# Sixteen buffers for row numbers and twenty for y in a fused convolution and mixture-of-experts kernel

## The chip, the cores and the metric

The kernel runs on one core of a Trainium2 chip. The metric is the device time of one execution in microseconds (us), the median of several runs; lower is better. The engines are named as in the profile: PE is TensorE (matmuls; PEld its weight loads), DVE is VectorE, ACT is ScalarE, POOL is GpSimd, SP (SPq) is SyncE, which here only issues DMAs.

## The reference

For 8 sequences of 3584 tokens with 192 features, a causal convolution of 7 taps with weights of its own for every token and head is computed, and its result goes through a mixture of 8 experts of which every token uses one:

```python
w = softmax(weight_gen)                                   # over the 7 taps
attn = einsum('bshk,bskhg->bshg', w, windows_of_7(x))     # 8 heads of 24
logits = attn @ w_gate                                    # 28672 tokens, 8 experts
e = argmax(logits); g = softmax(logits)[e]
out[token] = g * (relu(attn[token] @ w1[e]) @ w2[e])      # 192 -> 1024 -> 192
```

## The kernel before

The tokens are cut into 16 stages of 14 x 128. For a stage, `conv` (lines 344 to 365) multiplies and adds the 7 taps on VectorE, in instructions over half or all of a stage's rows. `tops` and `halves` (367 to 386) split the result into two f16 parts, which stand in one of three tiles `rows`. `turn`, `products`, `route1`, `counts` and `route2` work out the expert of each token and its place in a scratch table in DRAM, `scr`, in which the rows of an expert stand together. `scatter` (455) is a GpSimd DMA that writes 128 rows to their places, 14 of them a stage. `table` (489) makes from the counts a list of blocks of 256 rows of one expert that are complete; the stages 1 to 14 have 7 blocks each, the last one the rest.

A block is loaded by `load` (551), all of it issued from SyncE's queue in this order: the expert's weights w1 into one of three tiles `wt` (lines 560, 561), the block's rows transposed into one of three tiles `xb` (564), and its row numbers and gates into `mt` (570). The second half of the weights, w2, is issued by `seconds` (581) a little later, when the block before no longer needs that place. `Block.first` (596) multiplies by w1 on TensorE in four steps of two 128-column parts and `hh` is relu of that, on ScalarE (609). `low` (612) makes `hl`, what `hh` lost by rounding: for the early stages on TensorE and ScalarE (616, 617), later on VectorE (619). `second` (624) multiplies `hh` and `hl` by w2. `out` (639) writes each half of the block, 128 rows, with its gate into a tile `y` on ScalarE (642), and a GpSimd DMA (643) scatters it to the rows of the output that `mt` names. So a buffer of `mt` is free again, and one of `y` too, when that scatter has read it.

The order of the work on VectorE, ScalarE, TensorE and SyncE is written out by two generators, `produce` (the stages) and `consume` (the blocks), which a loop at the end of the kernel draws from by estimated times. GpSimd executes what it issues in order as well, so an output scatter can stand behind a stage's row scatters and the small operations of lines 327 to 180. The convolution ends about 1010 us into the span and the routing of the last stage about 1065 us; from there on TensorE runs through the blocks that are left.

Of the kernel before, what the change touches and what calls it, by code (L numbers as in the profile page):

```python
# [9 lines left out]
I32 = mybir.dt.int32  # L10
# [5 lines left out]
P = 128  # L16
# [32 lines left out]
TW0, TWE, TWU = 18.0, 8.0, 1.0  # L49
BLK, NEG = 16.6, 0.21  # L50
LAG2, LAG0, LAGN, LAGL = 2, 4, 1, 4
HHB, HLB, YB = 6, 6, 12
AV = 4.0
NZ = [0] * 5 + [5] * 1 + [8] * 10
FINE = 8
# [24 lines left out]
def conv_moe_kernel(ctx: ExitStack, tc: tile.TileContext, x, wgen, wg_in, w1, w2, out):  # L80
# [19 lines left out]
    def raw(i):  # L100
        return getattr(i, "ins", i)
# [346 lines left out]
    def no_dep(i, *groups):  # L448
        for g in groups:
            tc.declare_no_dep(i, group=g, reason="rows are disjoint")  # L450
# [94 lines left out]
    def written(i, s):  # L545

        info = mybir.DependencyInfo(mybir.DependencyClass.Sync, mybir.DependencyReason.DATA)
        for k in scats[s] + (zeros if s == nchunk - 1 else []):
            tc.add_manual_dep(i, k.name, info, reason="rows of the stage")

    def load(s, tb, g, bs):
        nj = bs // P
        ffn = pools[0]
        with tc.issue_after(loaded[-1]) if loaded else ExitStack():
            rv = SP.value_load(tb[0:1, 0, g:g + 1], min_val=0, max_val=TRASH + 256 - bs)
            ev = SP.value_load(tb[0:1, 1, g:g + 1], min_val=0, max_val=E - 1)
        wt = wts[len(loaded2) % len(wts)]
        loaded2.append(None)
        seconds()
        SP.dma_start(out=wt[:, F:4 * F], in_=wsc[bass.ds(ev, 1), :, F:4 * F].rearrange("o p c -> p (o c)"))  # L560
        SP.dma_start(out=wt[0:64, 0:F], in_=wsc[bass.ds(ev, 1), 0:64, 0:F].rearrange("o p c -> p (o c)"))
        xb = ffn.tile([P, 3 * 512], F16, name="xb", bufs=3)
        xv = xb[:, 0:3 * bs].rearrange("p (a b) -> p a b", a=3)
        i = raw(SP.dma_start_transpose(out=xv, in_=scr[bass.ds(rv, bs), 0:384]))
        later = [f"scat{k}" for k in range(s + 1, nchunk)] + ([] if s == nchunk - 1 else ["zero"])
        no_dep(i, *later)
        written(i, s)
        tc.add_to_no_dep_group("loads", i)
        mt = ffn.tile([P, 4, 2], I32, name="mt", bufs=8)
        i = raw(SP.dma_start(out=mt[:, 0:nj, :], in_=scri[bass.ds(rv, bs), 192:194].rearrange("(j p) c -> p j c", p=P)))  # L570
        no_dep(i, *later)
        written(i, s)
        tc.add_to_no_dep_group("loads", i)
        loaded.append(i)
        halfway.append((wt, ev))
        return wt, xv, mt

    def seconds():
        while halfway:
            wt, ev = halfway.pop(0)  # L580
            SP.dma_start(out=wt[:, 4 * F:WW], in_=wsc[bass.ds(ev, 1), :, 4 * F:WW].rearrange("o p c -> p (o c)"))
# [213 lines left out]
    def consume():  # L795
# [8 lines left out]
        def ahead(n, k):  # L804
            while len(ready) < k and n + len(ready) < len(todo):
                s, i, b, bs = todo[n + len(ready)]
                if s not in avail or (ready and t < avail[s]):
                    break
                ready.append(load(s, seg_tabs[s][i], b, bs))
# [28 lines left out]
        def rest(i):  # L838
            if i < len(skip):
                loaded.clear()  # L840
                with tc.If(cnt > skip[i][2]):
                    for s, j, b, bs in skip[i:i + NSS]:
                        blk = Block(load(s, seg_tabs[s][j], b, bs), bs, (0,) * NF)
                        seconds()
                        for k in range(blk.steps):
                            step(blk, k)
                        blk.gates()
                        step()
                    rest(i + NSS)
# [51 lines left out]
```

## Time and profile before

| | |
|---|---|
| median of 3 runs | 1263.31 us (1262.53 to 1265.07) |
| the profiled execution | 1258.3 us |
| its span, first to last instruction | 1256.6 us |
| busy in the span: PE, DVE, ACT, POOL | 1131.6, 1062.3, 708.1, 793.4 us |
| mean granted TensorE clock | 0.964 |

The rows in the section further down come from that one execution; times in them count from the start of its span. A row of a timeline has the start, the duration, the engine, the line of the kernel, the operation, what it writes and reads, how many instructions the row merges, and in brackets the idle time of the engine before it and what ended it. A row of waits has the engine and the line that waited, what it waited for, the total in us, the times, and the longest.

### The profile page before, as it was taken

What the parts mean: (1) busy time and instruction counts of PE and PEld (TensorE: products, weight loads), DVE (VectorE), ACT (ScalarE), POOL (GpSimd) and SP (SyncE); (2) the same over time, 40 slices, a digit from 0 to 9 for tenths busy, and PEclk for the clock granted to TensorE, in tenths of its full rate; (3) what the DMA queues carried; (4) which work ended last, traced back from release to release, by engine and by line L of the source; (5) the groups of instructions that cost most, each with busy time, mean ns of one, the idle gap of its engine ahead of it and who ended that gap; (6) DMA issues with size and microseconds to landing.
All of it is one profiled execution on the core that took longest, in us unless ns stands there. A gap on an engine that the chain in (4) does not pass through costs nothing.

```text
span 1256.6 us, 31171 instructions
## 1 busy us (share of the span) xinstructions
PE 1131.6 (90%) x11784; PEld 1014.4 (81%) x11784; DVE 1062.3 (85%) x1421; ACT 708.1 (56%) x1299; POOL 793.4 (63%) x611
## 2 busy tenths in 40 slices
PE   1485588999999998799999999999999999999997
PEld 0143277898887897689999999999989899999996
DVE  8998999999999999889999999999999865333332
ACT  5878664868776775545555455555544354333332
POOL 3227534658889897888878686886858563521222
PEclk9886798999999999999999999999999999999999
DMA  9749697998969969899999999999997999999992
GB/s 324 213 161 296 218 304 180 269 244 272 282 184 268 261 204 266 248 273 290 309 273 306 267 278 289 284 287 257 290 246 223 277 251 274 302 287 254 255 247 69
DMA packets 211946, 323.03 MB, mean 257 GB/s; under 512 B 138894, under 2 KB 158463, under 8 KB 209744
## 3 DMA queue, kind: packets, MB, share of 16 engines
q1 hardware_dynamic: 190000, 276.01, 78.8%
q0 software_dynamic: 21792, 44.99, 12.3%
q8 instruction: 94, 1.54, 0.5%
q14 instruction: 60, 0.49, 0.2%
HBM read 237.87 MB, written 61.03 MB: 238 GB/s over the span
## 4 chain that ended last, share of the span: by engine, by line
DVE 47%; PE 29%; DMA 9%; issue 7%; SPq 3%; ACT 3%; POOL 2%; POOLq 0%; DVEq 0%; ACTq 0%
DVE tmp L358 14%; DVE acc L363 14%; PE po L635 13%; DVE hl L619 5%; PE p L602 3%; PE p L606 3%; PE p L603 3%; PE p L605 3%; PE p L604 3%; DMA out_dram<-y,mt 3%; DVE acc L358 3%; DVE rows L384 3%; DMA xb<-scr 2%; DMA scr<-rows,pos 1%; DMA wt<-wsc 1%
## 5 line engine op out<-in xcount | busy, mean ns | idle before, releaser
L643 POOL DMA_INDIRECT out_dram<-y,mt x230 | 351.0, 1526 | 275.4 <-ACT y L642 215.9
L609 ACT ACTIVATE hh<-p 128x512 f16<-128x512 f32 x460 | 275.3, 599 | 391.4 <-PE p L606 376.0
L456 POOL DMA_INDIRECT scr<-rows,pos x224 | 360.9, 1611 | 121.5 <-issue 61.2
L635 PE MATMUL po<-wt,hh 128*128 128x192 f16 x3680 | 366.8, 249 | 0.0
L619 DVE SCALAR_TENSOR_TENSOR hl<-p,hh 128x512 f16<-128x512 f32 x334 | 225.1, 680 | 148.7 <-ACT hh L609 148.4
L635 PEld LDWEIGHTS <-hh 128*128 128x128 f16 x3680 | 316.2, 99 | 3.7
L363 DVE TENSOR_TENSOR acc<-acc,tmp 128x1344 f32<-128x1344 f32 (+1 forms) x168 | 290.7, 1747 | 1.0
L358 DVE TENSOR_TENSOR tmp<-xin,wgt 128x1344 f32<-128x1344 f32 (+1 forms) x168 | 290.6, 1746 | 0.9
L602 PE MATMUL p<-xb,wt 128*128 128x256 f16 x920 | 251.9, 274 | 39.3 <-DMA xb<-scr 32.4
L606 PE MATMUL p<-xb,wt 128*128 128x256 f16 x920 | 252.2, 274 | 0.0
L605 PE MATMUL p<-xb,wt 128*128 128x256 f16 x920 | 252.2, 274 | 0.0
L603 PE MATMUL p<-xb,wt 128*128 128x256 f16 x920 | 252.0, 274 | 0.0
L604 PE MATMUL p<-xb,wt 128*128 128x256 f16 x920 | 252.0, 274 | 0.0
L635 PE MATMUL po<-wt,hl 128*128 128x192 f16 x1840 | 228.8, 247 | 0.0
L635 PEld LDWEIGHTS <-hl 128*128 128x128 f16 x1840 | 165.3, 98 | 7.9
L602 PEld LDWEIGHTS <-wt 128*128 128x128 f16 x920 | 90.3, 98 | 42.4 <-issue 24.2
L603 PEld LDWEIGHTS <-wt 128*128 128x128 f16 x920 | 90.2, 98 | 29.6 <-issue 14.6
L399 ACT ACTIVATE xt<-p 128x1024 f16<-128x1024 f16 x96 | 86.5, 925 | 37.7 <-PE p L398 37.7
L617 ACT ACTIVATE hl<-p 128x512 f16<-128x512 f32 x126 | 75.7, 601 | 53.9 <-PE p L616 53.8
L604 PEld LDWEIGHTS <-wt 128*128 128x128 f16 x920 | 90.4, 98 | 11.0
L606 PEld LDWEIGHTS <-wt 128*128 128x128 f16 x920 | 90.4, 98 | 11.0
L605 PEld LDWEIGHTS <-wt 128*128 128x128 f16 x920 | 90.4, 98 | 11.0
(123 smaller groups left out, 1056.4 us busy)
## 6 DMA issues: line engine op xcount, KB each, us to landing
wt<-wsc SPq DMA_DIRECT2D x115, 768.5 KB
wt<-wsc SPq DMA_DIRECT2D x115, 768.0 KB
xin<-in_x_dram SPq DMA_DIRECT2D x15, 1344.0 KB
wt<-wsc SPq DMA_DIRECT2D x115, 128.0 KB
wgt<-in_weight_gen_dram SPq DMA_DIRECT2D x16, 392.0 KB
wsc<-wt SPq DMA_DIRECT2D x8, 768.5 KB
wa<-in_moe_w_dram SPq DMA_DIRECT2D x8, 768.0 KB
wa<-in_moe_w_dram SPq DMA_DIRECT2D x8, 512.0 KB
```

The lines of the kernel that those rows point to most:

```text
L358: V.tensor_tensor(out=t[:, a:b, :].rearrange("p t (h g) -> p (t h) g", g=G), in0=xv, in1=wv, op=ALU.mult)
L363: V.tensor_tensor(out=acc[:, a:b, :], in0=acc[:, a:b, :], in1=t[:, a:b, :], op=ALU.add)
L456: i = raw(GP.indirect_dma_start(scri, bass.IndirectOffsetOnAxis(ap=pos[:, t:t + 1], axis=0), rows_t[s % 3].bitcast(I32)[:, t, 0:RW // 2], ...
L602: PE.matmul(o, lhsT=wt[:, F + fs:F + fs + P], rhs=xv[:, 0, :], start=i == 0, stop=False)
L603: PE.matmul(o, lhsT=wt[:, F + fs:F + fs + P], rhs=xv[:, 1, :], start=False, stop=False)
L604: PE.matmul(o, lhsT=wt[:, 3 * F + fs:3 * F + fs + P], rhs=xv[:, 0, :], start=False, stop=False)
L605: PE.matmul(o, lhsT=wt[:, 2 * F + fs:2 * F + fs + P], rhs=xv[:, 2, :], start=False, stop=False)
L606: PE.matmul(o, lhsT=wt[:, fs:fs + P], rhs=xv[:, 2, :], start=False, stop=i == self.each - 1)
L609: A.activation(out=hh, in_=p1, func=AF.Relu, scale=1.0 - 2.0 ** -11 if self.via[k] else 1.0)
L619: V.scalar_tensor_tensor(out=hl, in0=p1, scalar=0.0, in1=hh, op0=ALU.max, op1=ALU.subtract)
L635: PE.matmul(o, lhsT=h[:, js], rhs=w2, start=(f == 0 and j % 2 == 0 and not part and w == 0), stop=part == 1 and f == NF - 1 and (j % 2 == ...
L643: i = raw(GP.indirect_dma_start(out, bass.IndirectOffsetOnAxis(ap=self.mt[:, j, 1:2], axis=0), y, None, bounds_check=N - 1, oob_is_err=False))
```

## The change

The pool of `mt` has 16 buffers instead of 8, and its tile is cut to the two halves that a block of 256 rows uses; the pool of `y` has 20 buffers instead of 12. Since a block takes one `mt` and two `y`, an `mt` is used again after 16 blocks instead of 8, and a `y` after 10 instead of 6.

```diff
-HHB, HLB, YB = 6, 6, 12
+HHB, HLB, YB = 6, 6, 20
...
-        mt = ffn.tile([P, 4, 2], I32, name="mt", bufs=8)
+        mt = ffn.tile([P, 2, 2], I32, name="mt", bufs=16)
```

The instructions of every engine and their order are the same in both kernels; what differs is what some of them wait for. On SyncE, the load of the thirtieth block, with the waits of each instruction (DMASW are landings of GpSimd's DMAs, DMAHW landings of SyncE's own):

```order
 L564 DMA_TRANSPOSE xb<-scr 128x3x256 [waits DMAHW4_49]
 L570 ISA
-L570 DMA mt<-scr 128x2x2 [waits DMAHW5_49,DMASW7_49,DMASW6_49]
+L570 DMA mt<-scr 128x2x2 [waits DMAHW5_49]
 L581 ISA
 L581 DMA wt_1138<-wsc 128x3074 [waits DMAHW6_49,PE_49,Activation_49]
```

The load of `mt` no longer waits for two output scatters. Of the 115 such loads, 95 name a scatter before and 18 after the change. On ScalarE, the two writes of `y` of one block:

```order
 L594 ACTIVATE g_6873<-mt,wt_1138 128x2 [waits DMAHW6_49,DMAHW5_49]
 L609 ACTIVATE hh<-p_6878 128x512 [waits PE_49,Activation_49]
-L642 ACTIVATE y<-po,g_6683 128x192 [waits DMASW0_49,PE_49,Activation_49]
-L642 ACTIVATE y<-po,g_6683 128x192 [waits DMASW1_49]
+L642 ACTIVATE y<-po,g_6683 128x192 [waits DMASW2_49,PE_49,Activation_49]
+L642 ACTIVATE y<-po,g_6683 128x192 [waits DMASW3_49]
 L617 ACTIVATE hl<-p_6854 128x512 [waits PE_49]
```

They still wait for output scatters, of ten blocks ago instead of six.

## Rows read from the trace of the kernel before

**Rows 1.** The first line of the page.

```profile
span 1256.6 us, 31171 instructions
```

**Rows 2.** The chain that ended last, in order of time: start us, us, what.

```profile
460.98 1.54 DVE acc L363
470.48 5.50 DMA out_dram<-y,mt
...
548.34 2.31 PE po L635 x28
...
591.20 2.31 PE po L635 x28
599.53 2.31 PE po L635 x28
...
740.17 2.00 DVE rows L384
...
954.62 5.46 DMA scr<-rows,pos
```

**Rows 3.** Busy time by stretch; the columns are in the first row.

```profile
core 0: us, PE busy (x) PEld busy (x) DVE busy (x) ACT busy (x) POOL busy (x), PEclk, DMA share, GB/s
460.00:480.00 20.00, 18.22 (x217) 16.61 (x215) 19.90 (x20) 12.85 (x23) 17.22 (x15) 1.00 0.55 156
500.00:520.00 20.00, 17.11 (x166) 15.13 (x164) 19.55 (x33) 11.42 (x21) 17.78 (x9) 0.96 0.79 185
520.00:540.00 20.00, 16.52 (x146) 14.72 (x145) 13.57 (x12) 7.61 (x14) 16.50 (x16) 0.79 1.14 320
720.00:820.00 100.00, 98.73 (x1093) 93.25 (x1091) 98.26 (x151) 52.09 (x100) 74.75 (x50) 1.00 1.03 285
820.00:920.00 100.00, 98.41 (x1133) 93.22 (x1133) 98.94 (x131) 52.67 (x100) 76.71 (x52) 1.00 0.98 279
```

**Rows 4.** VectorE's waits from 515 to 560 us.

```profile
DVE hl L619 <- ACT hh L609: 9.0, 6, 3.4
```

**Rows 5.** TensorE's waits from 470 to 548 us.

```profile
PE p L602 <- DMA xb<-scr: 10.4, 5, 3.5
PE p L602 <- DMA mt<-scr: 1.5, 1, 1.5
```

**Rows 6.** SyncE's waits from 440 to 720 us.

```profile
SPq L581 <- PE po L635: 49.6, 20, 5.3
SPq L570 <- DMA out_dram<-y,mt: 46.9, 8, 12.4
```

**Rows 7.** SyncE's queue, its order in time, near 460 us.

```profile
451.81 1.66 SPq L564 DMA_TRANSPOSE xb<-scr  x1
466.13 0.41 SPq L570 DMA_DIRECT2D mt<-scr  x1
```

**Rows 8.** GpSimd in order of time: the long hold, and the first and last of stage 7's 14 scatters.

```profile
445.80 17.58 POOL L643 DMA_INDIRECT out_dram<-y,mt  x1 [0.30 <-issue]
...
536.48 0.96 POOL L456 DMA_INDIRECT scr<-rows,pos  x1 [0.30 <-issue]
...
557.79 1.16 POOL L456 DMA_INDIRECT scr<-rows,pos  x1 [0.30 <-DMA mt<-scr]
```

**Rows 9.** VectorE in order of time, from 444 to 463 us.

```profile
444.71 3.01 DVE L358 TENSOR_TENSOR acc<-xin,wgt 128x1344 f32<-128x1344 f32 x2
...
459.51 3.01 DVE L363 TENSOR_TENSOR acc<-acc,tmp 128x1344 f32<-128x1344 f32 x2
462.45 0.95 DVE L305 TENSOR_REDUCE mx<-wgt 128x112 f32<-128x784 f32 x1
```

**Rows 10.** ScalarE's waits from 470 to 520 us.

```profile
ACT y L642 <- DMA out_dram<-y,mt: 4.0, 3, 2.9
```

**Rows 11.** SyncE's queue near 585 us: xb of the first block of stage 7.

```profile
584.92 2.19 SPq L564 DMA_TRANSPOSE xb<-scr  x1
```

**Rows 12.** GpSimd in order of time: the first and last of stage 4's 14 scatters.

```profile
337.24 6.01 POOL L456 DMA_INDIRECT scr<-rows,pos  x1 [0.30 <-issue]
...
375.08 2.68 POOL L456 DMA_INDIRECT scr<-rows,pos  x1 [0.31 <-issue]
```

## The prediction

> **What bounds the kernel now.** The span is 1256.6 us [rows 1]. I read the chain of waits first, then the busy time by stretch, then the waits of the engines that the chain passes through. The reader is to see in the chain that up to 461 us it lies on VectorE's convolution, that it then leaves VectorE for the landing of an output scatter (470 us), that from 548 to about 717 us it lies on TensorE, and that from 740 us it is VectorE's again [rows 2]. The busy time says the same: from 720 to 920 us VectorE works 197.2 of 200 us [rows 3], so nothing that only helps TensorE can shorten that stretch. The exception is 520 to 540 us, where VectorE works 13.57 of 20 us, TensorE 16.52, and the granted TensorE clock is 0.79, a mix of its full level and the half level (1.2 GHz of 2.4 GHz) [rows 3]. The kernel loses time on both engines at once there, and that is where the change acts.
>
> How that hole comes about is read backwards. VectorE waits six times for hh, 9.0 us in all [rows 4], because TensorE is late. TensorE waited 10.4 us for xb and 1.5 us for mt between 470 and 548 us [rows 5]. xb was late because SyncE's queue stood still: from 440 to 720 us it waited 46.9 us in 8 waits, up to 12.4 us, before the load of mt (line 570) for the landing of an output scatter [rows 6]. One is plain: xb of the thirtieth block is issued at 451.81 us, its mt not before 466.13 us [rows 7]; behind it in the same queue stand the second half of that block's weights and the next block's loads. The buffer of mt is free when the scatter of eight blocks ago has read it. GpSimd issues those scatters in order, and it was late: one of them held it for 17.58 us from 445.80 us [rows 8], exactly while VectorE ran conv and split instructions back to back; it came free when VectorE reached a reduction at 462.45 us [rows 9]. So a long run on VectorE ends, four engines later, as idle time on VectorE.
>
> By the Trainium skill (SBUF — State Buffer, Who interferes with whom) a VectorE instruction with two SBUF inputs contends with a GpSimd instruction that reads SBUF; the trace agrees with its 17.58 us. The same section reports that such an operation was not seen to stall DMAs issued by GpSimd, and infers that making descriptors does not need that port; by that the hold would not be there, and the measurement decides against it.
>
> **The change, part by part.** No instruction is added, removed or moved on any engine; only buffers, and with them waits, change.
>
> *Row numbers, 16 buffers instead of 8.* A load of mt now needs the scatter of sixteen blocks ago. Its longest wait, 12.4 us, is at most one and a half blocks of 8.33 us (599.53 less 591.20 us, one block after another on TensorE [rows 2]), so the scatter of eight blocks ago is there before ten blocks are over, and sixteen are never needed. I take all 46.9 us of SyncE's waits as gone. That is not 46.9 us of time: SyncE only has to keep ahead of TensorE. What it is worth is what was lost downstream. TensorE lost 10.4 + 1.5 = 11.9 us of waiting [rows 5], and in clock at most 0.04 x 20 + 0.21 x 20 = 5.0 us [rows 3], together at most 16.9 us. VectorE lost 9.0 us [rows 4]; the rest was a cushion, blocks that TensorE had done ahead. Since VectorE sets the pace both before the hole and from 740 us on [rows 2], the end moves by VectorE's loss, not TensorE's: **9.0 us**. What TensorE gains beyond it turns into waiting for hl. After the convolution TensorE alone runs to the end, from a start that moves with VectorE's, so nothing is given back there.
>
> *y, 20 buffers instead of 12.* ScalarE waited 4.0 us, 3 times, to write y while the scatter of six blocks ago had not landed [rows 10]. The longest, 2.9 us, lies inside the hole and its cost is already in the 9.0 us. Alone I cost it at nothing, but without it the same late scatters would hold the next blocks at y once mt no longer holds them; with twenty buffers the scatter may be ten blocks behind. A wait of 2.9 us at a distance of six blocks is over before the seventh, so ten are never needed either. I take it as the part that lets the 9.0 us through.
>
> *The hold itself* stays: the run on VectorE is the same. Nobody waits for it any more, except the scatters of a stage's rows behind it in GpSimd's queue. Those of stage 7 begin at 536.48 us and end at 558.95 us [rows 8], and the first block of that stage asks for its xb at 584.92 us [rows 11]. A scatter lands about 5.5 us after its issue [rows 2], so 564.4 us is the time to beat. If TensorE comes 9.0 us earlier the request comes at 575.9 us, if 16.9 us earlier at 568.0 us: both after it. So I cost this at 0.
>
> *Bounds.* Below, 0 (the transfers were bound otherwise); above, TensorE's whole 16.9 us. I take 9.0 us, because the row that speaks of the engine setting the pace is VectorE's.
>
> **Sum.** The profiled execution took 1258.3 us (its span and 1.7 us around it); less 9.0 us it is 1249.3 us. The three timed runs have a median of 1263.31 us, 5.0 us above the profiled one, all three within 2.6 us of each other; I move the median by the same 9.0 us: **1254.3 us**. About 0.2% (2.5 us) is what a measurement of this kernel can tell from no change.
>
> **The rivals.**
> *All of TensorE's loss comes back*, 16.9 us: 1246.4 us. For it: the timed runs are slower than the profiled one, so their hole may be larger. Against it: VectorE's 197.2 of 200 us.
>
> *Half of it comes back*, 4.5 us: 1258.8 us. The loads are issued earlier but xb still lands late, since at 520 to 540 us the DMA engines are busy at a share of 1.14 [rows 3]. Against it: that share is the catching up of a queue that had left them at 0.55 from 460 to 480 us [rows 3]; spread out, the same bytes fit, and 0.98 to 1.03 at 720 to 920 us costs hardly any wait.
>
> *Nothing comes back*: 1263 us. SyncE, let past mt, stops at the next thing in its queue: the second half of the weights (line 581) waits for TensorE to free one of three buffers, 49.6 us in 20 waits [rows 6], so the loads cannot run ahead and the change doesn't do what it says. Against it: such a wait ends when TensorE finishes a block, and so never starves it alone.
>
> *Slower*: GpSimd gets in between VectorE's long instructions; without VectorE's 9.0 us of idling it gets in less. If the 14 scatters of stage 7 then take what those of stage 4 took, 40.5 us from 337.24 to 377.76 us [rows 12] instead of 22.5 us, they land at 582.5 us, and 2.4 us are left of the gain. From 42.9 us on the first block of stage 7 comes later than now; with one more hold of 17.58 us they land at 600.1 us, 15.2 us late: 1278.5 us. For it: the same instructions of VectorE hold GpSimd at 445 us. Against it: in this stage VectorE writes hl, which reads PSUM, between them, and later stages, with VectorE full, issue their scatters without such holds.
>
> By the rule of that section (SBUF — State Buffer, Who interferes with whom, in the Trainium skill) whichever of the two engines starts first keeps the port for its instruction; that is this rival's mechanism, and the trace agrees in part: its 17.58 us lasted over twelve instructions of VectorE, not one [rows 9].
>
> **How the numbers follow.** The forecast has 0.60, all of it 0.09, half of it 0.12, nothing 0.12, slower 0.07. Faster by over 0.2% are the first three, 0.81; within 0.2% 0.12; slower 0.07. The range reaches from 1247 us, which leaves out the far end of the largest gain, to 1261 us, which takes in the half gain and leaves out no change and slower.
>
> **What would show it.** In the changed kernel SyncE's wait at line 570 for output scatters should be gone, the hold of GpSimd near 446 us still there, TensorE's waits for xb between 470 and 548 us under 3 us, its clock 1.00 at 500 to 560 us, and VectorE's wait for hh before the end of the convolution under 1 us. The chain should lie on VectorE from about 200 to 930 us without a break. If SyncE's wait is gone and TensorE's for xb is not, the loads were bound by something else; if both are gone and the span is not 9 us shorter, I have mistaken the engine that sets the pace; if TensorE waits for stage 7's rows, the slower rival is right.

## The result and the profile after

In the first comparison the changed kernel took 1245.67 us (median of 5 runs, 1244.87 to 1246.98) and the kernel before 1262.53 us (5 runs, 1252.88 to 1265.07): ratio 0.9888, 95% interval 0.985 to 0.9926. On the median of 1263.31 us that the prediction started from, that ratio is 1249.2 us. A later comparison (the second group below), with 12 and 35 runs, gave 1246.37 against 1254.45 us, ratio 0.994, interval 0.9915 to 0.9966. So the kernel is faster by 14.1 us (9.3 to 18.9) by the one and by 7.5 us (4.3 to 10.7) by the other; the changed kernel's medians agree, those of the kernel before don't. The forecast was 9.0 us. The profiled executions took 1258.3 us before and 1245.7 us after. Ratios and intervals come from the single runs, without those over 1.5% above the fastest of their kernel, so they need not be the ratios of the medians.

The first line of the page of the changed kernel [rows 1], and its windows [rows 3] with one more at 540 us:

```profile
span 1244.0 us, 31118 instructions
```

```profile
core 0: us, PE busy (x) PEld busy (x) DVE busy (x) ACT busy (x) POOL busy (x), PEclk, DMA share, GB/s
460.00:480.00 20.00, 19.80 (x247) 18.34 (x245) 19.86 (x20) 12.59 (x24) 16.93 (x16) 1.00 1.02 269
500.00:520.00 20.00, 19.39 (x204) 17.40 (x202) 19.76 (x26) 13.79 (x24) 18.29 (x8) 1.00 1.07 330
520.00:540.00 20.00, 17.67 (x212) 16.57 (x211) 19.93 (x22) 10.20 (x20) 16.82 (x15) 1.00 0.93 228
...
540.00:560.00 20.00, 17.76 (x206) 16.66 (x203) 19.79 (x26) 9.05 (x19) 16.34 (x13) 1.00 0.93 240
```

The hole is gone: VectorE works 19.93 us at 520 to 540 us where it had worked 13.57, and the granted TensorE clock is 1.00 where it had been 0.79. The DMA engines are no longer at 0.55 and then at 1.14, but at 1.02 and 0.93: the same transfers, spread out.

The waits of the changed kernel: the longest of SyncE's from 440 to 720 us [rows 6], and TensorE's from 200 to 1000 us; the last row is the kernel before in the same window.

```profile
SPq L581 <- PE po L635: 88.4, 27, 5.7
SPq L564 <- DMA scr<-rows,pos: 10.2, 2, 6.2
```

```profile
PE p L602 <- DVE hl L619: 8.0, 9, 2.2
...
PE p L602 <- DMA xb<-scr: 1.4, 1, 1.4
```

```profile
PE p L602 <- DVE hl L619: 4.7, 4, 2.0
```

Line 570 no longer waits there (in the whole execution it has 3.1 us of short waits left). SyncE waits instead at line 581 for the place of the second half of the weights, 88.4 us where it had been 49.6, and nothing downstream waits for that: between 470 and 548 us TensorE waits for no load, and from 440 to 600 us VectorE shows no wait [rows 4]. ScalarE's waits for `y` [rows 10] are gone too. TensorE now waits for VectorE's `hl` 8.0 us in 9 waits, where it had waited 4.7 us in 4. One wait is new: SyncE stands 4.0 us at line 564 for a stage's row scatters between 500 and 560 us, and TensorE doesn't feel it.

GpSimd of the changed kernel in order of time [rows 8], and SyncE's line 564, the request of `xb` for the first block of stage 7 [rows 11]:

```profile
444.30 17.57 POOL L643 DMA_INDIRECT out_dram<-y,mt  x1 [0.30 <-issue]
462.17 0.98 POOL L643 DMA_INDIRECT out_dram<-y,mt  x1 [0.30 <-issue]
...
538.58 0.96 POOL L456 DMA_INDIRECT scr<-rows,pos  x1 [0.30 <-DVE sm L339]
...
559.57 1.76 POOL L456 DMA_INDIRECT scr<-rows,pos  x1 [0.30 <-issue]
```

```profile
L564 SPq DMA_TRANSPOSE xb<-scr x1: 1436/1436/1436, 573.0 to 573.0; - x1
```

The hold of 17.57 us is untouched. Stage 7's scatters end at 559.57 + 1.76 = 561.3 us; with the 5.5 us that a landing took [rows 2] that is 566.8 us, and the request comes at 573.0 us.

The chain of the changed kernel [rows 2], in order of time:

```profile
335.73 6.01 POOL scr L456
...
443.27 2.94 DVE acc L358 x2
...
547.64 2.94 DVE acc L363 x2
...
665.12 2.93 DVE acc L363 x2
676.46 2.31 PE po L635 x28
...
705.74 5.97 DMA out_dram<-y,mt
...
728.91 2.00 DVE rows L384
```

Through the stretch where it had left VectorE (461 to 717 us), it now stays on it from 443 to 665 us. It leaves it for stretches of some 50 us from 676 and from 748 us, again from 920 us, and from 283 to 443 us, where both kernels run the same and the chain before lay on VectorE. Two chains that differ over the same work say that there more than one path is close to the longest.

Where the 12.6 us between the two spans lie is read from the start of three blocks on TensorE. The rows are line 602 in narrow windows (the first of the two times is the start): block 21, 56 and 84, counted from 0, before and then after.

```profile
L602 PE MATMUL p<-xb,wt x2: 269/271/273, 383.0 to 383.6; 128*128 128x256 f16 x2
...
L602 PE MATMUL p<-xb,wt x2: 272/272/273, 722.9 to 723.4; 128*128 128x256 f16 x2
...
L602 PE MATMUL p<-xb,wt x2: 269/271/273, 977.8 to 978.3; 128*128 128x256 f16 x2
```

```profile
L602 PE MATMUL p<-xb,wt x2: 270/272/273, 381.5 to 382.0; 128*128 128x256 f16 x2
...
L602 PE MATMUL p<-xb,wt x2: 272/272/273, 711.6 to 712.1; 128*128 128x256 f16 x2
...
L602 PE MATMUL p<-xb,wt x2: 272/272/273, 963.7 to 964.2; 128*128 128x256 f16 x2
```

Up to block 21 the changed kernel is 1.5 us ahead, from 21 to 56 it gains 9.8 us (339.9 against 330.1), from 56 to 84 another 2.8 us (254.9 against 252.1), and from there to the end it loses 1.5 us. The change can act only from about 440 us on, so the 1.5 us is not its work. The 2.8 us goes with the scatters of stage 13: their times part at one of them, beside VectorE's multiplication of line 358. GpSimd and VectorE before:

```profile
954.62 2.36 POOL L456 DMA_INDIRECT scr<-rows,pos  x1 [0.30 <-issue]
```

```profile
954.60 1.54 DVE L358 TENSOR_TENSOR tmp<-xin,wgt 128x1344 f32<-128x1344 f32 x1
```

and after:

```profile
943.30 0.96 POOL L456 DMA_INDIRECT scr<-rows,pos  x1 [0.30 <-issue]
944.56 1.16 POOL L456 DMA_INDIRECT scr<-rows,pos  x1 [0.30 <-issue]
```

```profile
943.28 1.61 DVE L358 TENSOR_TENSOR tmp<-xin,wgt 128x1344 f32<-128x1344 f32 x1
```

In both VectorE starts 0.02 us earlier by the record. Before, the scatter takes 2.36 us; after, it takes 0.96 us and VectorE's instruction 0.07 us longer. From there on the two engines' times differ, and the stage's 14 scatters take 23.4 instead of 29.0 us. In a second execution of the same changed kernel they took 29.8 us and the stretch from block 56 to 84 its 254.9 us again; it is 254.9 to 255.0 us in every profile of the first two groups below but that of six buffers (254.1 us). So these 2.8 us are an accident of that execution, and the change's own part is the stretch from block 21 to 56.

### The profile page after: what moved, and what is told of

Its sections match the earlier page's. It is cut to its first block, busy times and chain, and to the rows that moved or that the text cites. A ratio compares the mean times of both kernels' runs of the same rounds, so it can differ in the third digit from the quotient of the medians.

```text
span 1244.0 us, 31118 instructions
## 1 busy us (share of the span) xinstructions
PE 1124.9 (90%) x11784; PEld 1010.1 (81%) x11784; DVE 1061.7 (85%) x1421; ACT 707.8 (57%) x1299; POOL 797.3 (64%) x611
## 3 DMA queue, kind: packets, MB, share of 16 engines
q0 software_dynamic: 21792, 44.99, 12.6%
## 4 chain that ended last, share of the span: by engine, by line
DVE 47%; PE 29%; issue 7%; DMA 7%; POOL 5%; ACT 3%; SPq 0%; POOLq 0%; DVEq 0%; ACTq 0%
DVE tmp L358 13%; PE po L635 13%; DVE acc L363 12%; DVE hl L619 7%; POOL scr L456 3%; PE p L602 3%; PE p L606 3%; PE p L605 3%; PE p L604 3%; PE p L603 3%; DMA out_dram<-y,mt 3%; DVE acc L358 3%; DVE rows L384 3%; DMA scr<-rows,pos 2%; POOL out_dram L643 2%
## 5 line engine op out<-in xcount | busy, mean ns | idle before, releaser
L643 POOL DMA_INDIRECT out_dram<-y,mt x230 | 345.8, 1504 | 270.1 <-ACT y L642 210.6
L606 PEld LDWEIGHTS <-wt 128*128 128x128 f16 x920 | 90.4, 98 | 10.8
L605 PEld LDWEIGHTS <-wt 128*128 128x128 f16 x920 | 90.3, 98 | 10.8
L604 PEld LDWEIGHTS <-wt 128*128 128x128 f16 x920 | 90.2, 98 | 10.8
```

Source lines behind the costliest of these rows:

```text
L604: PE.matmul(o, lhsT=wt[:, 3 * F + fs:3 * F + fs + P], rhs=xv[:, 0, :], start=False, stop=False)
L605: PE.matmul(o, lhsT=wt[:, 2 * F + fs:2 * F + fs + P], rhs=xv[:, 2, :], start=False, stop=False)
L606: PE.matmul(o, lhsT=wt[:, fs:fs + P], rhs=xv[:, 2, :], start=False, stop=i == self.each - 1)
L643: i = raw(GP.indirect_dma_start(out, bass.IndirectOffsetOnAxis(ap=self.mt[:, j, 1:2], axis=0), y, None, bounds_check=N - 1, oob_is_err=False))
```

## The experiments

The theory is the prediction's: VectorE sets the pace, and the time moves by what VectorE idles between 440 and 600 us, because `mt` had too few buffers while GpSimd was late. The rivals are that it moves by TensorE's larger loss, that the buffers of `y` matter more, and that GpSimd's hold can be had out of the way instead. Three groups ran on chips of their own, a last run on a fourth.

### First group: the parts of the change, on one chip

The kernel before had a median of 1254.07 us there (25 runs, 1248.81 to 1258.94).

**Row numbers alone** (`y` stays at 12):

```diff
-        mt = ffn.tile([P, 4, 2], I32, name="mt", bufs=8)
+        mt = ffn.tile([P, 2, 2], I32, name="mt", bufs=16)
```

> Sixteen buffers of row numbers, y left at twelve. My theory (the waits at mt start the hole, y would take their place): SyncE's waits at line 570 for output scatters from 440 to 720 us fall from 46.9 us to under 1 us, but ScalarE now waits at y for scatters, some 10 us instead of 4.0 us; about two thirds of the gain, 1248 to 1253 us. Rival (y plays no part): the same time as the changed kernel, 1245.7 us within 1.5 us, and ScalarE's waits at y stay at 4 us. Rival (the y buffers carry the gain): as before, 1259 to 1265 us.

Measured: 1248.84 us (6 runs), ratio 0.9939 (0.9915 to 0.9963). Line 570 shows no wait from 440 to 720 us. ScalarE's waits for `y` in that stretch, and VectorE's from 440 to 600 us:

```profile
ACT y L642 <- DMA out_dram<-y,mt: 10.3, 6, 2.2
```

```profile
DVE hl L619 <- ACT hh L609: 1.8, 3, 1.3
```

As foreseen the late scatters now hold ScalarE at `y`, 10.3 us instead of 4.0 [rows 10] (5.7 us in the kernel before on this chip). But of VectorE's wait only 1.8 us is left: most of the gain goes through without the larger `y`.

**y alone** (`mt` as before):

```diff
-HHB, HLB, YB = 6, 6, 12
+HHB, HLB, YB = 6, 6, 20
```

> Twenty buffers of y, row numbers left at eight. My theory: the waits at line 570 stay at 40 to 50 us and with them the hole; no change against before beyond its own spread, 1255 to 1263 us. Rival (the y buffers carry the gain): 1246 to 1250 us.

Measured: 1255.25 us (12 runs), ratio 1.0004 (0.9985 to 1.0023): no difference. SyncE's wait is what it was, and VectorE's is 6.4 us:

```profile
SPq L570 <- DMA out_dram<-y,mt: 51.2, 8, 12.6
```

**Ten and fourteen buffers**, the least that the prediction's words allow ("before ten blocks are over" for `mt`, "over before the seventh" for `y`):

```diff
-HHB, HLB, YB = 6, 6, 12
+HHB, HLB, YB = 6, 6, 14
...
-        mt = ffn.tile([P, 4, 2], I32, name="mt", bufs=8)
+        mt = ffn.tile([P, 2, 2], I32, name="mt", bufs=10)
```

> Ten buffers of row numbers and fourteen of y. The prediction said that the scatter waited for is there before ten blocks are over and, for y, before the seventh block: then this is as fast as the changed kernel, 1245.7 us within 1.5 us, with no wait at line 570 over 1 us. Rival (the scatters fall further behind once nobody holds the blocks back): some waits of 2 to 8 us return at line 570 or at y and the time lies between, 1248 to 1256 us.

Measured: 1247.26 us (8 runs), ratio 0.9948 (0.9928 to 0.9968): the whole gain, as far as the runs can tell. SyncE's and ScalarE's waits from 440 to 720 us:

```profile
SPq L570 <- DMA out_dram<-y,mt: 10.8, 5, 5.7
```

```profile
ACT y L642 <- DMA out_dram<-y,mt: 0.7, 1, 0.7
```

The expectation that line 570 would not wait over 1 us fell: it waits five times, up to 5.7 us. A queue let past one wait runs further ahead and asks earlier for the next buffer, so the length of a wait seen before doesn't tell how many buffers take it away. The load of block 36 shows it, here and in the kernel before:

```profile
511.41 1.28 SPq L564 DMA_TRANSPOSE xb<-scr  x1
```

```profile
532.43 1.31 SPq L564 DMA_TRANSPOSE xb<-scr  x1
```

Its request comes 21.0 us earlier, of which 4.2 us is the start of block 21 in that execution (378.8 against 383.0 us). GpSimd was done with the scatter of ten blocks ago at 512.25 us, against 516.56 us before: 4.3 us earlier, no more than that start. The wait costs nothing here, since SyncE is far ahead: VectorE waits 0.4 us in all.

**The kernel before, again**, to see what two executions of it differ by:

> The kernel before once more, for the size of its hole in another execution. Its five timed runs lie between 1252.9 and 1265.1 us, those of the changed kernel between 1244.9 and 1247.0 us. My theory: the difference between executions of the kernel before is the hole itself, so in this profile VectorE's wait for hh from 500 to 600 us differs from 9.0 us by about as much as the span differs from 1256.6 us. Rival: the spread comes from elsewhere (the first 160 us, the clock, the end) and the hole is 9.0 us again within 1 us.

Measured: 1254.41 us (10 runs), ratio 0.999 (0.9971 to 1.0009). Its profiled span is 1251.3 us, 5.3 us under the first one's 1256.6 us. VectorE's wait is 6.9 us instead of 9.0, which is 2 of the 5.3; 4.7 us lie before block 21, which starts at 378.3 instead of 383.0 us, and 1.2 us come back after block 84. So the size of the hole differs between executions, but it isn't the main part of their spread.

### Second group: the hold, and fewer buffers, on another chip

The kernel before had a median of 1254.45 us there (35 runs, 1246.47 to 1265.58).

**The changed kernel, again:**

> The changed kernel once more, on one chip with the kernel before in the same rounds. The first comparison had 16.9 us between the medians, the profiles 12.6 us, the stretch from the first matmul of the 22nd block to that of the 57th 9.8 us. My theory: the change is worth the hole, 8 to 10 us between medians on one chip (1244 to 1247 us against 1254 us if the chip is that of the second group of runs), and the rest of the 16.9 us was the chip or the minutes in which the earlier runs of the kernel before were taken. Rival: the change is worth 14 us or more wherever both run together.

Measured: 1246.37 us (12 runs), ratio 0.994 (0.9915 to 0.9966). Its profiled span is 1244.0 us, as in the first comparison, though stage 13 took the long way; its block 21 starts at 378.0 us. Beside the kernel before of the first group (378.3 us, span 1251.3 us) it is 7.3 us shorter, and 7.2 us of that lie between blocks 21 and 56 (338.1 against 330.9 us).

**The kernel before with VectorE's run broken**, by writes of 0.27 us between pairs of half-row instructions in stage 8:

```diff
-    big = ctx.enter_context(tc.tile_pool(name="big", bufs=2))
+    big = ctx.enter_context(tc.tile_pool(name="big", bufs=2)); gap = const.tile([P, 255], F32, name="gap")
...
-                    n += 1
+                    n += 1; c == FINE and k < 3 and i and V.memset(gap, 0.0)
...
-                        n += 1
+                        n += 1; c == FINE and k < 3 and i and V.memset(gap, 0.0)
```

> The kernel before, buffers 8 and 12, with five memsets of 128 x 255 between the pairs of VectorE's run at 445 us (stage 8 of the convolution), so that GpSimd can get in; nothing else on VectorE changes. My theory (the one hold of 17.58 us makes GpSimd late, that makes SyncE stand at line 570): no output scatter over 5 us between 440 and 465 us, SyncE's waits at line 570 from 440 to 720 us fall from 46.9 us to under 20 us, VectorE's wait for hh from 9.0 or 7.1 us to under 3 us, and the time falls by 4 to 8 us, less some 1.4 us for the memsets. Rival (GpSimd is late from its whole load in stages 3 to 5, and one hold more or less does not matter): the hold goes, but the waits at line 570 stay over 35 us and the time stays within 2 us.

Measured: 1251.8 us (12 runs), ratio 0.9982 (0.9958 to 1.0005). GpSimd and the writes on VectorE, in order of time:

```profile
442.84 9.05 POOL L643 DMA_INDIRECT out_dram<-y,mt  x1 [0.30 <-issue]
...
454.45 6.77 POOL L643 DMA_INDIRECT out_dram<-y,mt  x1 [0.19 <-issue]
...
462.80 5.36 POOL L643 DMA_INDIRECT out_dram<-y,mt  x1 [0.30 <-issue]
```

```profile
444.75 0.27 DVE L359 MEMSET gap<- 128x255 f32 x1
...
447.90 0.27 DVE L359 MEMSET gap<- 128x255 f32 x1
...
451.04 0.27 DVE L364 MEMSET gap<- 128x255 f32 x1
```

A scatter of the kernel before, beside the pair of line 358 beside which the third of these stands:

```profile
465.06 5.11 POOL L643 DMA_INDIRECT out_dram<-y,mt  x1 [0.19 <-issue]
```

The edit did only a part of what it was for. The hold of 17.6 us became two of 9.05 and 6.77 us; the 5.36 us are no part of it, since the kernel before has 5.11 us at that pair. The first scatter passes after the third opening (451.04, it ends at 451.89 us). Counted from the start of the half-row instructions (444.71 us before, 441.74 us here), it is through 8.5 us earlier than before, but the fifth scatter behind it only 2.1 us earlier. Line 570 still waits 54.7 us. With the hold shortened and not gone, the run doesn't decide whether the hold is the cause.

**Six buffers of row numbers:**

```diff
-        mt = ffn.tile([P, 4, 2], I32, name="mt", bufs=8)
+        mt = ffn.tile([P, 2, 2], I32, name="mt", bufs=6)
```

> Six buffers of row numbers instead of eight, y at twelve: the suspected wait made larger. My theory: two blocks fewer make each late scatter hold SyncE some 16 to 20 us more, waits at line 570 begin at about 300 us instead of 446 us, come to over 150 us in all, and VectorE's wait for hh to 25 us or more: slower by 15 to 40 us. Rival (the waits at line 570 are harmless, the weights' buffers bound the loads): within 3 us of before.

Measured: 1260.79 us (10 runs), ratio 1.0052 (1.002 to 1.0084): slower by 6.5 us (2.5 to 10.5), not by 15 to 40. VectorE waits 13.8 us from 440 to 600 us, most of it (9.4 us) for ScalarE's `rows` of line 372 and only 2.2 us for `hh`. SyncE's waits at line 570 from 440 to 720 us, and in the whole execution:

```profile
SPq L570 <- DMA out_dram<-y,mt: 70.4, 10, 23.3
```

```profile
SPq L570 <- DMA out_dram<-y,mt: 118.4, 22, 23.3
```

In the kernel before the whole execution has 54.7 us of them and none from 290 to 440 us; with six buffers waits of 22.9 us (93.3 us from 290 us on, less the 70.4) are already done by 440 us. So 63.7 us more of waiting (not the 95 us and more that were foreseen) cost 6.5 us: most of it falls where SyncE is ahead.

**The changed kernel with the broken run** (its two lines, and the same writes):

> The changed kernel, buffers 16 and 20, with the same five memsets. My theory: with enough buffers nobody waits for the held scatter, so taking the hold away gains nothing and the memsets cost what they take on VectorE: 0 to 2 us slower than the changed kernel. Rival (the hold still costs, through the stage's row scatters behind it): 1 to 4 us faster than the changed kernel.

Measured: 1247.59 us (10 runs), ratio 0.9931 (0.9903 to 0.996): no better than the changed kernel, 1.2 us above it in the medians, and VectorE has five instructions more. GpSimd's times are those of the other broken run (9.05, 6.77 and 5.37 us), so here too the hold was shortened and not taken away.

### Third group, and the last run: the hold taken away

Stage 8 is computed in whole-row instructions, as stages 1 and 5 to 7 are, each of which needs the one before it:

```diff
-FINE = 8
+FINE = 9
```

This went into the kernel before (e9) and the changed kernel (e10); e11 is the changed kernel again, and e12 repeats e9.

> The kernel before, buffers 8 and 12, with stage 8 of the convolution in instructions over all its rows, 2.9 us each, as in stages 5 to 7, instead of halves; the memsets let GpSimd take one step each, and a scatter takes three, so they did not remove the hold. Between whole instructions a scatter took 2.7 us (411 to 440 us). My theory (the hold makes the hole): no output scatter over 4 us between 440 and 465 us, GpSimd some 13 us earlier from then on, SyncE's waits at line 570 from 440 to 720 us under 20 us instead of 46.9 to 55.5 us, VectorE's wait for hh under 2 us, and the time 5 to 8 us under before. Rival (GpSimd is late from all of stages 3 to 5 and the hold adds little): the waits at line 570 stay over 35 us and the time within 2 us of before.

> The changed kernel, buffers 16 and 20, with stage 8 over whole rows. My theory: nobody waits for the hold any more, so the time is that of the changed kernel within 2 us. Rival (the hold still costs through the row scatters behind it): 2 to 5 us faster than the changed kernel.

> The changed kernel beside the two before it, on one chip with the kernel before. My theory: 7 to 10 us under the median of before, as in the second comparison (8.1 us). Rival: 14 us or more, as in the first.

> The kernel before, with stage 8 computed in whole-row instructions instead of half-row ones, as the third group tried it. The theory is that line 570's waits come from GpSimd's 17.6 us hold beside VectorE's twelve back-to-back half-row instructions: without that stretch no output scatter between 440 and 465 us should take over 6 us, line 570 should wait under 20 us in all between 440 and 720 us (46.9 before), VectorE's waits on hh should be under 2 us (9.0 before), and the time 5 to 8 us under the kernel before, up to 2 us of it given back by the longer instructions. The rival is that eight buffers are simply too few for GpSimd's whole load in stages 8 and 9, hold or no hold: line 570 then waits over 35 us, and the time is within 2 us of the kernel before.

The times decide nothing. On both chips every kernel was some 100 us slower than elsewhere (the kernel before 1361.35 us in 24 runs, 1331.01 to 1389.82, and 1354.55 us in 11, 1312.63 to 1384.02); e9 took 1355.13 us (ratio 1.0103, 1.0013 to 1.0194), e10 1360.67 us (0.9994, 0.9918 to 1.0069), e11, the changed kernel itself, 1356.71 us (1.0064, 0.9994 to 1.0134), e12 1348.05 us (1.0215, 1.0093 to 1.0336). ScalarE stood still there for something that the profile doesn't name, in e12:

```profile
ACT hh L609 <- remote: 130.1, 18, 21.4
```

No profile of the first comparison or of the first two groups shows such a wait. VectorE's waits on `hh`, foreseen under 2 us, came to 20.6 us in e9 and 12.4 us in e12; the changed kernel, whose line 570 doesn't wait there, has 12.8 us on the same chip as e9 (e11), so here they don't measure the hold. The order of GpSimd's work can still be read. At the place of the hold, in e12 and then in e11, where stage 8 is in half rows, and SyncE's wait in e12 from 440 to 720 us:

```profile
451.80 5.57 POOL L643 DMA_INDIRECT out_dram<-y,mt  x1 [0.30 <-issue]
```

```profile
451.09 11.33 POOL L643 DMA_INDIRECT out_dram<-y,mt  x1 [0.30 <-issue]
```

```profile
SPq L570 <- DMA out_dram<-y,mt: 23.4, 4, 19.1
```

In whole rows no scatter there takes over 5.57 us (e9: 5.56 us, e10: 5.57 us); in half rows, on the chip of e9 and e10, one takes 11.33 us. So the hold does come with the back-to-back half-row instructions, though it is not always 17.6 us long. Line 570 waits 23.4 us (e9: 17.9 us) where the kernel before waited 46.9 us in the first comparison: from 440 to 485 us it is 3.5 us (e9: 2.9 us) for 17.4 us. The larger part of what is left is one wait at about 500 us, of 19.1 us (e9: 12.9 us): there output scatters stand behind the 14 row scatters of a stage in GpSimd's order. By these figures the hold makes about half of the waits, and GpSimd's order the rest. That is an estimate across chips: the kernel before was not profiled on these two. What the hold alone is worth in time stays open.

## Why the prediction was right, and where it was not

**The waits go, the end moves by VectorE's loss.** Right, and it is the best tested step. From block 21 to 56 VectorE has the same work in every kernel, so the length of that stretch less its busy time is what it idles. Busy time by window, that stretch alone, of the kernel before, the changed kernel, `mt` alone and six buffers:

```profile
383.00:722.90 339.90, 324.39 (x3554) 300.13 (x3554) 325.03 (x436) 193.09 (x361) 279.60 (x187) 0.98 0.99 272
```

```profile
381.50:711.60 330.10, 320.61 (x3554) 297.00 (x3555) 324.39 (x436) 192.68 (x361) 283.00 (x186) 1.00 1.02 280
```

```profile
382.90:715.20 332.30, 322.59 (x3554) 299.20 (x3555) 324.65 (x436) 193.12 (x361) 279.89 (x187) 0.99 1.00 278
```

```profile
381.90:727.10 345.20, 325.13 (x3554) 301.11 (x3555) 325.54 (x438) 192.89 (x361) 263.62 (x188) 0.98 0.97 268
```

| kernel (buffers of mt, y) | stretch, us | DVE busy | the rest | of it DVE's waits in the stretch |
|---|---|---|---|---|
| six (6, 12) | 345.2 | 325.5 | 19.7 | 13.8 |
| before (8, 12) | 339.9 | 325.0 | 14.9 | 9.1 |
| before, again | 338.1 | 325.3 | 12.8 | 7.1 |
| y alone (8, 20) | 337.6 | 325.0 | 12.6 | 6.8 |
| mt alone (16, 12) | 332.3 | 324.7 | 7.6 | 1.8 |
| ten (10, 14) | 330.6 | 324.5 | 6.1 | 0.4 |
| changed, again (16, 20) | 330.9 | 324.8 | 6.1 | 0.4 |
| changed (16, 20) | 330.1 | 324.4 | 5.7 | 0 |

VectorE's work stays within 1.1 us over eight profiles, and the stretch follows its idle time; less the waits that the profile names, the rest is 5.7 to 5.9 us in every row. From the kernel before to the changed one the rest falls by 9.2 us, from the second pair by 6.7 us; the waits on `hh` that the prediction read were 9.0 [rows 4] and 6.9 us. The rival with TensorE's whole loss of 16.9 us falls with it: TensorE's waits for loads went, but from 440 to 720 us its waits fell only from 12.9 to 6.9 us, since 5.2 us of them are now for `hl`, where 0.8 us had been. The first comparison's medians also differ by 16.9 us, but its profiles do not show that in this stretch.

**The size.** 9.0 us lies in the interval of the second comparison (4.3 to 10.7 us), and just under that of the first (9.3 to 18.9 us). The changed kernel's median of 1245.67 us is 8.6 us under the forecast of 1254.3 us. The step at fault is the one from the profile to the median: "I move the median by the same 9.0 us" took 1263.31 us as the kernel's time. Two chips with 25 and 35 runs gave 1254.07 and 1254.45 us; from there 9.0 us less is 1245.1 and 1245.5 us. Three runs within 2.6 us of each other were no proof against another level in other runs: two more of the same comparison gave 1252.88 and 1259.31 us. Nor can a measurement tell 0.2% from nothing here: the two intervals reach 0.4% and 0.3% to either side. Why the first runs were high isn't settled; one thing that differs between executions without the change is the start of block 21 (378.3 and 383.0 us). From the profiled execution the sum gave 1249.3 us; 1245.7 us came out, 0.8 us of the 3.6 us short in the stretch of the hole (9.8 for 9.0), 1.5 before it, 2.8 with stage 13, and 1.5 us back at the end. So a part of what the first comparison's profiles show beyond the forecast is chance, in both directions.

**Sixteen are never needed.** Right in effect, wrong in its reason. "The scatter of eight blocks ago is there before ten blocks are over" took a wait's length for the distance; with ten buffers line 570 still waits 10.8 us, up to 5.7, because the requests come earlier.

**y, "the part that lets the 9.0 us through".** Mis-sized. Without it `mt` alone brings the rest of that stretch from 12.8 us (the kernel before, same chip) to 7.6 us; a larger `y` brings at most a further 1.5 us (6.1 us with ten and fourteen). In time the runs can't tell the two apart (0.9939 and 0.9948, with intervals that overlap). That `y` alone is worth nothing held (1.0004, 0.9985 to 1.0023).

**The hold stays and costs nothing.** It stays, 17.57 us at 444.30 us, and nothing is seen to wait for it: line 570 doesn't, and shortening it in the changed kernel gained nothing. No run outside the third group and the last run took it away altogether. Stage 7's scatters came 6.2 us before they were asked for (573.0 less 566.8 us), so the slower rival had no ground; the 4.0 us that SyncE waited for row scatters between 500 and 560 us, which the prediction left out, reached no other engine. That the hold ends when VectorE reaches a reduction holds for this one and not in general: in e11 it ended at 462.42 us, within the two split instructions of line 384.

**Nothing comes back because line 581 holds the loads.** The wait was there and grew, 88.4 for 49.6 us, and as the prediction said against this rival it starved nobody: TensorE waited for no load from 470 to 548 us.

**The signs.** Line 570 without a wait, the hold still there, no wait of TensorE for `xb` from 470 to 548 us, the clock at 1.00 from 500 to 560 us, no wait of VectorE for `hh`: all came. The chain "on VectorE from about 200 to 930 us without a break" did not; it stays there from 443 to 665 us, and leaves VectorE before and after.

**The rule on the port.** By the Trainium skill (SBUF — State Buffer, Who interferes with whom) the engine that issues first keeps the shared port for its instruction. The race in stage 13 agrees in part: in one execution the scatter took 2.36 us, 1.4 us longer than free, beside an instruction of VectorE that had started 0.02 us earlier. In the other, where the scatter got its 0.96 us, VectorE lost 0.07 us and not the length of the scatter, and by the record it had again started first. The section's inference that making descriptors doesn't need the port that a two-input instruction takes is against the holds here, 17.57, 9.05 and 6.77 us.

## What to carry to other kernels

When a queue of loads stands at a buffer that another engine's late work has to free, price it by what the engine that sets the pace idles, not by the queue's wait: here 46.9 us of waiting were worth 7 to 10 us in the stretch, and with six buffers 63.7 us more of it 6.5 us. A wait's length doesn't say how many buffers take it away, since the queue runs further ahead once it is gone; try the depth. Before a gain of a per cent is added to a median of three runs, look at how far two executions of the same kernel lie apart, and in which stretch.

## What the runs showed that was not expected

An indirect scatter of GpSimd can be held over many instructions of VectorE, and what lets it through stays open. Free, it takes 0.96 to 0.99 us. With writes of 0.27 us between pairs of half-row instructions it passed after the third, 9.05 us after its start, and the hold of 17.58 us ended with VectorE's reduction of 0.95 us [rows 9]; that looked as if a scatter had to collect its time from several openings. But in the broken run the next scatter (452.20 us) took only 1.84 us beside the two split instructions of line 384, and in e11 the held one ended beside them, without a write or a reduction before it. No run varied the opening's length.

Such a hold is rare: in the kernel before no other scatter took over 6.70 us, though stages 2 to 4 and those from 9 on are in half-row instructions too. In whole rows no output scatter at that place took over 5.57 us, and several took 2.7 us.

The same program took 1254 us on two chips and 1361 and 1355 us on two others, where ScalarE's waits for something outside the profile came to over 100 us (130.1 us in 18 waits). There the change made no difference that could be measured (e11).
